# Six small loads in place of two for one input vector of a decode kernel on one core

## The chip, the cores and the metric

The kernel runs on one core of a Trainium2 chip. Its time is the device time of one execution in microseconds (us). A profiled execution also has a span: from its first instruction to its last. The core has five engines with instruction streams of their own: PE (matrix products), DVE (vector operations), ACT (activation functions), POOL and SP. Data is moved by 16 DMA engines; SP and ACT each have one DMA queue (q1 is SP's, q10 is ACT's), and one load of several rows is spread over the DMA engines. A load tells that it has landed by counting up a semaphore.

## The reference, cut to what matters

One token is decoded: attention over a cache with 32 query heads on 4 key/value heads, beside a small two-layer mixer with an MLP; both read the normalised input and are added to the input.

```python
x  = A_x                                   # (1, 1, 1024), bf16
xn = layernorm(x)
q  = (xn @ wq)                             # 32 heads of 128
p  = softmax(q k^T * 128**-0.5)            # 4 key/value heads, 65536 keys each
A  = (p v) @ wo                            # wq: 1024 x 4096, wo: 4096 x 1024
h  = gelu(layernorm(xn) @ w1)              # four groups of channels shifted along the sequence,
x1 = xn + shifted(h) @ w2                  # which has length 1
B  = x1 + gelu(layernorm(x1) @ w3) @ w4    # w3: 1024 x 3584, w4: 3584 x 1024
out = x + A + B                            # (1, 1, 1024)
```

Keys and values are 4 x 65536 x 128 bf16 each. Together with the weights some 170 MB are read once; nothing of it is read twice.

## The kernel before, in words

**Items and slots.** Everything large goes through three slots of 64 KB per partition (pool `big`, `SLOTS = 3`). The list `items` (lines 83 to 89) holds the order: wq, K(0,0), V(0,0), w3, w12 (that is w1 and w2 in one slot), then K and V of the remaining halves of each key/value head, w4 ahead of the last V, and wo in three items. K(g,r) is half r of head g: 32768 keys, 256 per partition, so that one load has 128 rows of 65,536 bytes. The loop of lines 440 to 442 computes item i after it has issued the loads up to item i+2 (`ensure`, `LOOKAHEAD = 2`). All these loads stand in SP's stream (line 119), in the order of the list. A load into a slot waits until the item that had the slot before is consumed: w3 waits for wq's products (line 242), w12 for K(0,0)'s, K(0,1) for V(0,0)'s products (line 393), V(0,1) for w3's, K(1,0) for w12's. A scheduling layer derives these waits from the tiles that each instruction reads and writes; within an engine it keeps the order of issue.

**Semaphores of the loads.** The same layer gives DMAs eight semaphores in turn, in the order in which it meets them. A DMA whose semaphore was used before waits for the earlier DMA on it, unless its engine is known to have waited for that already. At the end SP waits for all of them, two per instruction, in a fixed order (line 468), and then for the other engines.

**The start.** ACT issues two loads of the vector x, ahead of everything else it does: line 123 loads it as 128 rows of 8 elements into `x_bf`; line 130 loads it again as 4 rows of 256 elements into partitions 0, 32, 64 and 96 of `x_q`, which is a part of the tile `work`. That load waits for the memset of line 129. `ones_f`, a matrix of ones, is another part of the same tile, filled by POOL on line 147; the layer takes the four-row load and this memset for overlapping, so that the memset waits for the load. `layernorm` (lines 168 to 188) is a chain over DVE, PE and ACT: the sum over partitions is a product with `ones_f` (lines 172 and 181). It is done twice, the second time on the first one's result. Between the two, DVE does line 199, which scales `x_q`, the only reader of `x_q`; PE adds its result to the accumulator `psB` on line 201. In DVE's stream line 199 stands ahead of lines 174 to 187 of the second layernorm, and in PE's stream line 201 stands ahead of line 181 of the second layernorm and of the products with wq (line 242).

**A key/value half.** `compute_K`: DVE transposes the slot in place in four pieces (line 337), PE multiplies with the queries (line 340), DVE, PE and DVE find the maximum (lines 344 to 355), ACT takes the exponential (line 357), DVE transposes it (line 359). `compute_V`: PE multiplies with the values (line 393). w3 and w12 are computed after V(0,0).

**The end.** The last products with wo go into `psB` (line 161), DVE copies it out (line 435), and SP stores 4 rows of 512 bytes (line 436).

Of the kernel before, what the change touches and what calls it, by code (L numbers as in the profile page):

```python
# [22 lines left out]
def kernel(  # L23
# [14 lines left out]
    nc = tc.nc  # L38
    P = 128
# [8 lines left out]
    DC = D // P  # L48
# [10 lines left out]
    NQ = NOUT // 4  # L59
# [33 lines left out]
    def work():  # L93
        return ppool.tile([P, HF * 512], BF16, name="work")[:]
# [25 lines left out]
        st[item] = t  # L120

    x_bf = const.tile([P, DC], BF16, name="x_bf")
    nc.scalar.dma_start(out=x_bf[:], in_=A_x[0, 0, :].rearrange("(p c) -> p c", c=DC))
    wk0 = work()
    qrow = wk0[:, 0:1024].rearrange("p (b n) -> p b n", b=2)
    psel = wk0[:, 1024:1536].rearrange("p (b m) -> p b m", b=4)
    x_q = wk0[:, 1536:1536 + NQ]
    ones_f = wk0[:, 1792:2048].bitcast(F32)
    nc.vector.memset(x_q, 0.0)
    nc.scalar.dma_start(out=x_q[0:P:32, :], in_=A_x[0, 0, :].rearrange("(j n) -> j n", j=4))  # L130

    n_issued = [0]

# [34 lines left out]
    def layernorm(src, tag):  # L168
# [50 lines left out]
                          in_=sel8[:].unsqueeze(2).to_broadcast([P, 8, 4]))  # L219

    iv = ident_bf[:].rearrange("p (b i r) -> p b r i", b=2, r=2)
    for b in range(2):
        for par in range(2):
            nc.vector.tensor_copy(out=psel[:, 2 * b + par, :].rearrange("p (a i) -> p a i", a=4),
                                  in_=iv[:, b, par, :].unsqueeze(1).to_broadcast([P, 4, 32]))
# [4 lines left out]
                          in_=lead.unsqueeze(2).to_broadcast([P, 4, 16]))  # L230
    gsel = const.tile([P, P], BF16, name="gsel")
    nc.vector.tensor_copy(out=gsel[:].rearrange("p (j m) -> p j m", j=2),
                          in_=lead[:, 0:2].unsqueeze(2).to_broadcast([P, 2, 64]))
# [239 lines left out]
```

## Time and profile before

| | before |
|---|---|
| median of 3 runs | 402.89 us (402.79 to 403.63) |
| the profiled execution | 402.66 us |
| its span | 400.9 us, so 1.8 us lie around it |
| read from memory | 169.87 MB, 424 GB/s over the span |
| busy: PE / DVE / ACT / POOL | 204.0 / 209.0 / 27.3 / 5.9 us |
| mean granted clock of PE | 0.796 |

The busy times are shares of one span of 400.9 us, spread over stages with different limits; the page of the profile also gives the chain of work that ended last, the span in 40 slices, the DMA queues with their packets, and per load the time from its issue to its landing. Line numbers are those of the kernel before; in the changed kernel everything after the first load stands one to three lines lower down.

### The profile page before, as it was taken

The numbers are of one execution on the slowest core, as the hardware profiler recorded it, in microseconds if no ns is written. First come the engines' busy times: TensorE is split into PE (matmuls) and PEld (weight loads), VectorE is DVE, ScalarE is ACT, GpSimd is POOL, SyncE is SP. The second block draws the span as 40 slices with busy tenths as digits, with TensorE's granted clock in tenths as the row PEclk, the third lists the DMA queues.
The fourth block names the chain that finished last, engine by engine and source line by source line (L and its number), as shares of the span: only waits on it lengthen the run. The fifth ranks groups of instructions, "written<-read, shape, count | busy, mean of one in ns | idle before, by whom it ended". The sixth has DMA issues, their size and how long they took to land.

```text
span 400.9 us, 3366 instructions
## 1 busy us (share of the span) xinstructions
PE 204.0 (51%) x1489; PEld 85.4 (21%) x1489; DVE 209.0 (52%) x190; ACT 27.3 (7%) x33; POOL 5.9 (1%) x27
## 2 busy tenths in 40 slices
PE   0016393660079148741965295529453935496235
PEld 0003131220023013310322042204121412143113
DVE  0022992230196559634954894279358841885120
ACT  0002002110000300020002000100200020002000
POOL 1010000000000000000000000000000000000000
PEclk9999698695569587967895689679975976599588
DMA  9999999999999999999999999999999999999994
GB/s 406 425 425 419 419 420 452 401 489 419 425 433 419 419 484 427 419 432 438 420 419 471 432 420 438 438 420 438 451 419 425 433 445 436 419 455 419 414 416 174
DMA packets 3773, 170.07 MB, mean 424 GB/s; under 512 B 552, under 2 KB 560, under 8 KB 816
## 3 DMA queue, kind: packets, MB, share of 16 engines
q1 hardware_dynamic: 3608, 169.87, 98.1%
q8 instruction: 11, 0.18, 0.2%
q10 hardware_dynamic: 152, 0.00, 0.0%
q14 instruction: 2, 0.02, 0.0%
HBM read 169.87 MB, written 0.00 MB: 424 GB/s over the span
## 4 chain that ended last, share of the span: by engine, by line
DMA 48%; PE 26%; DVE 20%; ACT 4%; issue 1%; ACTq 0%; SPq 0%; POOL 0%; DVEq 0%
DMA slot<-in_A_k_cache_dram 28%; PE sc L340 14%; DVE slot L337 12%; DMA slot<-in_A_v_cache_dram 10%; PE oacc L393 8%; DMA work<-in_A_x_dram 7%; DMA slot<-in_A_wo_dram 3%; DVE work L359 3%; DVE mx L344 3%; ACT work L357 3%; PE rows L242 1%; ACT L357 1%; PE pm_mx L346 0%; DVE m L348 0%; DVE og L408 0%
## 5 line engine op out<-in xcount | busy, mean ns | idle before, releaser
L340 PE MATMUL sc<-slot,qst 128*128 128x512 bf16 x512 | 129.8, 415 | 75.6 <-DVE slot L337 75.6
L337 DVE STREAM_TRANSPOSE slot<-slot 128x4096 f32<-128x4096 f32 x32 | 139.4, 4413 | 49.4 <-DMA slot<-in_A_k_cache_dram 49.3
L340 PEld LDWEIGHTS <-qst 128*128 128x128 bf16 x512 | 52.1, 103 | 152.1 <-DVE slot L337 55.9
L393 PE MATMUL oacc<-slot,work 128*32 128x512 bf16 x512 | 43.3, 513 | 45.3 <-DVE work L359 35.7
L344 DVE TENSOR_REDUCE mx<-sc 128x1 f32<-128x2048 f32 x8 | 18.3, 2292 | 30.2 <-PE sc L340 30.2
L393 PEld LDWEIGHTS <-work 128*32 128x32 bf16 x512 | 16.3, 124 | 69.2 <-DVE work L359 36.3
L357 ACT ACTIVATE work<-sc,nball 128x2048 bf16<-128x2048 f32 x8 | 15.7, 1967 | 193.5 <-DVE nball L355 193.5
L359 DVE STREAM_TRANSPOSE work<-work 128x2048 bf16<-128x2048 bf16 x8 | 18.5, 2311 | 19.1 <-ACT work L357 19.1
L408 DVE SCALAR_TENSOR_TENSOR og<-oacc,wm,og 128x128 f32<-128x128 f32 x16 | 5.6, 351 | 22.2 <-PE oacc L393 21.8
L172 PE MATMUL pm_ln<-ln_rowsum_a,work 128*128 128x1 f32 x2 | 0.6, 362 | 27.7 <-POOL work L147 27.7
L166 DVE CAST xT<-x_bf 128x8 f32<-128x8 bf16 x1 | 0.2, 172 | 22.0 <-DMA x_bf<-in_A_x_dram 22.0
L346 PE MATMUL pm_mx<-ident_f,mx 128*1 128x128 f32 x8 | 2.3, 283 | 18.1 <-DVE mx L344 18.1
L242 PE MATMUL rows<-slot,xpad 128*32 128x512 bf16 (+1 forms) x144 | 9.6, 397 | 0.9 <-DMA slot<-in_B_w_dram 0.9
L161 PE MATMUL psB<-slot,oT 128*1 128x256 bf16 x128 | 6.3, 362 | 6.3 <-DMA slot<-in_A_wo_dram 6.1
L357 ACT ACT_TABLE_LOAD x2 | 2.6, 1283 | 73.5 <-DVE nball L355 73.5
L287 DVE TENSOR_TENSOR work<-pm_h,mask 128x448 f32<-128x448 f32 x1 | 0.6, 625 | 11.4 <-PE pm_h L284 11.4
L172 PEld LDWEIGHTS pm_ln<-ln_rowsum_a,work 128*128 128x128 f32 x2 | 0.5, 310 | 27.6 <-POOL work L147 27.6
L435 DVE CAST work<-psB 97x256 bf16<-97x256 f32 x1 | 0.4, 425 | 11.4 <-PE psB L161 11.4
L161 PEld LDWEIGHTS <-oT 128*1 128x1 bf16 x128 | 3.9, 108 | 8.8 <-issue 5.6
L242 PEld LDWEIGHTS <-xpad 128*32 128x32 bf16 x144 | 4.4, 103 | 5.7 <-DMA slot<-in_B_w_dram 1.8
L346 PEld LDWEIGHTS pm_mx<-ident_f,mx 128*1 128x1 f32 x8 | 0.6, 79 | 21.9 <-DVE mx L344 21.9
L412 PE MATMUL pm_e<-og,sel8x 128*32 128x129 f32 x8 | 1.6, 282 | 6.6 <-DVE og L408 6.6
(102 smaller groups left out, 65.4 us busy)
## 6 DMA issues: line engine op xcount, KB each, us to landing
slot<-in_B_w_dram SPq DMA_DIRECT2D x2, 7168.0 KB, 37.7
slot<-in_A_wo_dram SPq DMA_DIRECT2D x1, 5120.0 KB, 27.0
slot<-in_B_w_dram SPq DMA_DIRECT2D x2, 2048.0 KB, 23.1
slot<-in_A_wo_dram SPq DMA_DIRECT2D x1, 2048.0 KB, 26.3
slot<-in_A_wo_dram SPq DMA_DIRECT2D x1, 768.0 KB, 13.5
slot<-in_A_wo_dram SPq DMA_DIRECT2D x1, 256.0 KB
slot<-in_A_k_cache_dram SPq DMA_DIRECT2D x8, 41.7
slot<-in_A_v_cache_dram SPq DMA_DIRECT2D x8, 38.6
```

The lines of the kernel that those rows point to most:

```text
L161: nc.tensor.matmul(psB[32 * j:32 * j + 1, 0:NQ], lhsT=lhsT, rhs=w_row[:, NQ * j:NQ * (j + 1)], start=False, stop=False, tile_position=(0, ...
L172: nc.tensor.matmul(pm[:, 0:1], lhsT=ones_f, rhs=rowsum[:], start=True, stop=True)
L242: nc.tensor.matmul(acc[32 * j:32 * j + 32, bk, 0:width], lhsT=xp[:, c, :], rhs=wt[:, c, ch * width:(ch + 1) * width], start=(c == 0), stop ...
L337: nc.vector.transpose(out=kf[:, cg, :], in_=kf[:, cg, :])
L340: nc.tensor.matmul(sc[:, hf, :], lhsT=qst[g % 2][:, bp, 24 - 8 * cg:24 - 8 * cg + P], rhs=kr[:, cg, hf, :, bp // 2, :, bp % 2], start=(cg ...
L344: nc.vector.reduce_max(out=mx[:], in_=sc[:].rearrange("p h n -> p (h n)"), axis=AX.X)
L346: nc.tensor.transpose(pm[0:1, 0:P], mx[:, 0:1], ident_f[:])
L357: nc.scalar.activation(out=pT, in_=sc[:], func=ACTF.Exp, bias=nball[:, r:r + 1], scale=SCALE, accum_out=lall[:, r:r + 1])
L359: nc.vector.transpose(out=pT, in_=pT)
L393: nc.tensor.matmul(oacc[32 * u:32 * (u + 1), :], lhsT=pT[:, hf, 32 * t:32 * (t + 1)], rhs=vt[:, :, hf, t, :], start=(hf == 0 and t < 4), s ...
L408: nc.vector.scalar_tensor_tensor(out=og[:, 0:P], in0=oacc[:, P * cg:P * (cg + 1)], scalar=wm[:, 1, cg:cg + 1], in1=og[:, 0:P], op0=ALU.mul ...
L412: nc.tensor.matmul(pe[rows, 0:P + 1], lhsT=sel8x[:], rhs=og[:], start=True, stop=True, tile_position=(0, 32 * g))
```

## The change

The load of `x_bf` is split into two loads of 64 rows, and the load of `x_q` into four loads of one row each. The bytes, their source and their places are the same. All six are issued by ACT, in the order written.

```diff
     x_bf = const.tile([P, DC], BF16, name="x_bf")
-    nc.scalar.dma_start(out=x_bf[:], in_=A_x[0, 0, :].rearrange("(p c) -> p c", c=DC))
+    for hp in range(2):
+        nc.scalar.dma_start(out=x_bf[64 * hp:64 * hp + 64, :],
+                            in_=A_x[0, 0, 512 * hp:512 * hp + 512].rearrange("(p c) -> p c", c=DC))
...
     nc.vector.memset(x_q, 0.0)
-    nc.scalar.dma_start(out=x_q[0:P:32, :], in_=A_x[0, 0, :].rearrange("(j n) -> j n", j=4))
+    for j in range(4):
+        nc.scalar.dma_start(out=x_q[32 * j:32 * j + 1, :], in_=A_x[0, 0:1, NQ * j:NQ * (j + 1)])
```

In the built program no instruction of PE, DVE, POOL or SP is added, removed or moved. What differs beside the six loads are the waits. The store is the 28th DMA before and the 32nd after, so it counts on the eighth semaphore in place of the fourth; the loads of SP's stream shift by four places in the same way. The third load of SP's stream, V(0,0), now waits for the first half of `x_bf`; w1 waits for the second half, w2, K(0,1), V(0,1) and K(1,0) for the four rows of `x_q`, one each. Line 166 waits for two loads, line 199 for four. POOL's memset of line 147 no longer waits for a load.

## The prediction

> **What bounds the kernel now.** I read first the slices and the DMA queues of the page.
>
> ```profile
> DMA  9999999999999999999999999999999999999994
> DMA packets 3773, 170.07 MB, mean 424 GB/s; under 512 B 552, under 2 KB 560, under 8 KB 816
> q1 hardware_dynamic: 3608, 169.87, 98.1%
> q10 hardware_dynamic: 152, 0.00, 0.0%
> ```
>
> The DMA engines are busy in every slice, 98.1% of the span for SP's queue alone: the kernel ends when 170 MB have been moved, and a delay of compute costs nothing until SP's queue runs dry. Then every idle microsecond of the DMA engines is lost. So two questions decide: when do the small loads land, and does a late one let q1 run dry?
>
> The packet counts say how loads are cut. q1 has 25 loads and a store: 25 x (128 rows + 16) + 4 + 4 = 3608, so each row is one packet and each DMA engine that takes part adds one for the semaphore. q10: 128 + 16 for `x_bf`, 4 + 4 for `x_q` (on four engines): 152.
>
> Next, the issues of the first 2 us with their time to landing, and the chain of waits.
>
> ```profile
> x_bf<-in_A_x_dram ACTq DMA_DIRECT2D x1, 2.0 KB, 22.3
> slot<-in_A_wq_dram SPq DMA_DIRECT2D x1, 22.1
> ```
>
> ```profile
> 1.18 26.16 DMA work<-in_A_x_dram
> 27.34 0.05 issue
> 27.39 0.21 POOL work L147
> 27.61 0.04 issue
> 27.65 0.60 PE pm_ln L172 x2
> ...
> 34.44 4.48 PE rows L242 x64
> ```
>
> 2 KB need 22.3 us, as long as the 8 MB beside them. The trace's packet records say why: on each DMA engine a packet of q10 goes only between two packets of q1. One engine's 16-byte packets start at 4.83, 7.25, 9.67, 12.09, 14.53, 16.95, 19.37 and 21.79, behind the eight 65,536-byte packets of wq, which take 2.42 us each. Its ninth, the semaphore, goes at 21.80, directly behind wq's own semaphore packet, which is short. `x_q`'s rows follow at 24.34 to 24.57 and their semaphores at 26.78 to 27.02, behind the first and second packet of K(0,0); they land at 27.34. So a q10 packet costs one **turn** of 2.42 us, and turn n goes behind the n-th packet of q1.
>
> ```profile
> 32.40 0.40 DVE L199 TENSOR_SCALAR work<-work,ln_s,ln_s 128x256 f32<-128x256 bf16 x1
> 32.99 1.20 PE L201 MATMUL psB<-work,ident_f 128*128 128x256 f32 x2
> 33.98 0.46 PE L181 MATMUL pm_ln<-ln_rowsq_b,work 128*128 128x1 f32 x2
> 34.37 4.50 PE L242 MATMUL rows<-slot,xpad 128*32 128x512 bf16 x64
> ```
>
> This timeline shows what stands behind `x_q`: line 199 at 32.40, and 2.0 us later the products with wq, which cannot pass line 201 in PE's stream.
>
> Last, SP's own timeline and the chain from the first V onwards.
>
> ```profile
> 38.94 25.26 SPq L119 DMA_DIRECT2D slot<-in_B_w_dram  x3
> 78.67 0.33 SPq L119 DMA_DIRECT2D slot<-in_A_k_cache_dram  x1
> 82.75 0.33 SPq L119 DMA_DIRECT2D slot<-in_A_v_cache_dram  x1
> ```
>
> The tightest place is K(0,1), issued at 78.67, when V(0,0) is consumed. The load queued ahead of it, w2, ends on the 16 DMA engines between 87.14 and 88.72 by the packet records. All other issues have more ahead of them: w3 (38.94) has V(0,0) in flight to 61, w12 (63.4) has w3 to 78, later ones 10 us and more.
>
> **The change part by part.**
>
> *The x_bf halves.* 64 rows over 16 engines are 4 packets and a semaphore: turns 1 to 5 and 6 to 10. Turn 10 goes behind K(0,0)'s first packet, at 24.3 on most engines and 25.0 on the last; with 0.4 us from packet to landing the second half lands near 25.4 in place of 23.0. The memset of line 147 no longer waits, so the first product with ones starts near 25.8 instead of 27.65: 1.9 us are gained here, and they are worth nothing, because line 199 is late next.
>
> *The x_q rows.* Each is one row and one semaphore. No row of this trace shows on which engine a one-row load goes. From one side: all on one engine (or each cut over all 16), 8 turns, 11 to 18. From the other: four engines side by side, turns 11 and 12, landing near 29.6. I take the first, since the loads stand in one queue in the order written and the four rows of one load before took four engines in order. Turn 17 goes behind K(0,0)'s eighth packet, which ends between 41.12 and 41.86, and turn 18 directly behind its short semaphore packet. With 0.3 us to landing: 41.9, against 27.34.
>
> The Trainium skill (DMA: Bandwidth & Descriptors, Why a DMA increments its semaphore by 16 and not by 1) has a load that is not split over all engines run on the lowest-numbered ones, which would put four one-row loads on the same engine.
>
> *What x_q holds up.* Line 199 starts at 41.9, not 32.40: 9.5 us late. Behind it on DVE stand the second layernorm's lines; in 2.0 us, as before, PE gets to the products with wq. K(0,0) landed at 42.19, just when DVE was ready for it (line 337 at 42.24), so nothing later absorbs the delay: the chain from line 242 to V(0,0)'s last product moves as it is. ACT waits for four more semaphores ahead of its first line 357; at 0.07 us for two of them that is 0.1. K(0,1) is issued at 78.67 + 9.5 + 0.1 = 88.3.
>
> *q1 runs dry.* From issue to moving: wq was issued at 0.74 and its first packets ended between 4.83 and 5.59, so less 2.42 they moved effectively 1.67 to 2.43 us after issue. The engine that gets dry first (87.14) is the one at 1.67; it moves again at 88.3 + 1.7 = 90.0, a loss of 2.8 us. It matters that this engine ended late: the packet records show three DMA engines at the end at 396.79 to 396.97, each having done two 16 KB fetches of instructions on the way (0.9 us each); the other thirteen end 0.9 to 2.9 us sooner. Two of the three had their first fetch ahead of 87 us and get dry at 88.7, losing only 1.3; the third is the one above. End: 396.79 + 2.8 = 399.6 against 396.97: **+2.6 us**.
>
> *New waits in SP's stream.* V(0,0) waits for the first half of `x_bf`: turn 5 is 14.5, landing 15. Behind it in SP's stream is w3, which isn't due before 48, and the engines have K(0,0) until 41: nothing. w1 waits for the second half, w2 and the next three for `x_q`'s rows, all landed by 42 and these loads due from 72 on: nothing. If that cover were gone, dry time would be the price, 1 for 1.
>
> *The store's semaphore.* SP's five waits at the end stand 0.066 us apart (399.81 to 400.07), and the store's is in the first of them before, in the last after. Four pass ahead of the landing: **-0.26 us**. The six issues on ACT (0.40 for the first one of before, 1.04 for the second) end by some 6 us at most, and only `x_bf`'s halves have a turn by then: nothing.
>
> Sum: 402.66 + 2.6 - 0.26 = **405.0 us**. The profiled execution is 0.23 us under the median of the runs shown, so beside that median it reads 405.2; I keep 405.0.
>
> Bounds: the delay of 9.5 is 9.3 to 10.0 (which engine takes the rows). Restart is 1.03 us (the first packet's start after its issue) to 2.43. The lost time is 1.3 if the two engines that are late anyway set the end, and 3.9 with the late ends of both. So 403.7 to 406.3, and 0.5 more on top for PE's clock: 403.7 to 406.8.
>
> **The rivals.**
>
> *Side by side.* The four rows go to four engines. `x_q` lands near 29.6, line 199 starts near 30.6 on the gained 1.9 us, and nothing is late. In general all is covered while K(0,1) is issued before 87.14 - 1.7 = 85.5, 6.7 us of delay after the 0.1 on ACT: `x_q` landing before 39.1. Then only the tail counts: 402.4, not slower. For it: the one load of four rows did run on four engines at once. Against it: it was one load.
>
> *Turns hold several packets.* If the DMA engines took several small packets in one turn, six loads would need six turns, be there by 20, and the time would be 402.4 too. Against it: all 152 packets of q10 went one per turn.
>
> The Trainium skill (DMA: Bandwidth & Descriptors, Queues, rings and completion order) has each DMA engine go round its queues and drain a whole packet, typically 9 to 17 descriptors, per visit; by that, `x_bf` before would have landed near 5. The trace differs (22.3 us).
>
> The same page (Anatomy of one DMA) gives some 2.0 us fixed per load; four more loads would then bring `x_q` to an estimated 35.3, and the time to 402.4. The trace has 4.3 us between the two landings (23.02 and 27.34).
>
> *V(0,0) held past K(0,0).* Were the first half of `x_bf` to land after 41.3 - 1.7 = 39.6, q1 would be dry there as well: a landing at 42 costs 2.4, together 407.4. Against it: turn 5.
>
> *The dry time made good later.* The slices rule this out: there is no idle DMA time from which to make it good.
>
> **How the numbers follow.** Forecast 0.68; side by side 0.14; several packets or a smaller fixed price 0.08; V(0,0) held or a longer stall 0.07; else 0.03. About 0.2% (0.8 us) is what a measurement of this kernel can tell from no change. The forecast's own range is 403.7 to 406.8; with 0.22 at 402.4, the range has to take those in: 402.3 to 406.8. Faster by over 0.2% has only the rest and scatter: 0.04. Within: 0.22 and the edge of the forecast: 0.23. Slower: 0.73.
>
> **What would show it.** q10 would have 168 packets (288 if each row is cut over 16 engines). `x_q`'s last row lands near 42, line 199 and the products with wq are 9.5 us later, while the first product with ones is 1.9 us earlier. V(0,0) is issued near 15, K(0,1) near 88, and the slice there falls below 9. I would be wrong if line 199 starts before 39, or if K(0,1)'s landing isn't later than 108.42.

## The result, and the profile after

The changed kernel takes 408.16 us (median; 407.76 to 409.14), the kernel before 402.86 us in the same comparison (402.79 to 403.63): a ratio of 1.0132, 95% interval 1.0117 to 1.0147. It is slower by 5.3 us, on the side that was forecast, but above the range, where the prediction had put 0.07 for a longer stall. The profiled execution took 408.03 us, with a span of 406.1 us and a mean granted clock of 0.802.

The page of the changed kernel, slices and DMA queues:

```profile
DMA  9999998969999999999999999999999999999994
DMA packets 3789, 170.07 MB, mean 419 GB/s; under 512 B 568, under 2 KB 576, under 8 KB 832
q1 hardware_dynamic: 3608, 169.87, 97.3%
q10 hardware_dynamic: 168, 0.00, 0.0%
```

q10 has 16 packets more, the semaphores of the second half. The bytes are the same and the mean rate is lower: the DMA engines stood still somewhere, and the 6 in the slices puts it between 81 and 92 us.

The chain of waits of the changed kernel around `x_q` (start us, us, what):

```profile
3.23 40.87 DMA work<-in_A_x_dram
...
44.22 0.42 DVE work L202
...
44.69 1.22 PE psB L204 x2
...
46.13 4.81 PE rows L245 x64
```

Line 202 is line 199 of before. It started at 32.40 and now starts at 44.22, released by the last row of `x_q`, which lands at 44.09. SP's own timeline shows what follows from it:

```profile
17.73 0.33 SPq L119 DMA_DIRECT2D slot<-in_A_v_cache_dram  x1
50.95 25.25 SPq L119 DMA_DIRECT2D slot<-in_B_w_dram  x3
90.84 0.33 SPq L119 DMA_DIRECT2D slot<-in_A_k_cache_dram  x1
```

K(0,1) is issued at 90.84 instead of 78.67. By the packet records the load ahead of it (w2) ends on the 16 DMA engines between 87.66 and 89.54, and K(0,1)'s first packets start at 91.81 to 92.20. In between q1 is dry. How much the DMA engines moved in the 40 us around this is read from the table by stretch (us, busy time of PE, PEld, DVE, ACT and POOL, clock, DMA share, GB/s). Before:

```profile
60.00:100.00 40.00, 16.59 (x197) 6.98 (x195) 8.97 (x11) 6.72 (x7) 0.53 (x1) 0.76 1.02 441
```

and after:

```profile
60.00:100.00 40.00, 26.77 (x211) 10.98 (x209) 20.27 (x13) 6.72 (x7) 0.52 (x1) 0.84 0.93 383
```

58 GB/s less over 40 us are 2.32 MB, and at the mean of 424 GB/s of the kernel before that is 5.5 us. This is rough, since the view counts a packet whole where it starts (so the DMA share can read 1.02). With each packet shared out over its duration the records give 432 GB/s before and 375 after, which is 5.3 us. The store lands 5.45 us later (405.24, 399.79 before). So the whole loss arises here, and nothing later gives any of it back.

### The profile page after: what moved, and what is told of

Read it like the earlier page. It is cut to its first block, busy times and chain, and to the rows that moved or that the text cites. A ratio compares the mean times of both kernels' runs of the same rounds, so it can differ in the third digit from the quotient of the medians.

```text
span 406.1 us, 3376 instructions
## 1 busy us (share of the span) xinstructions
PE 206.6 (51%) x1489; PEld 86.7 (21%) x1489; DVE 208.7 (51%) x190; ACT 27.3 (7%) x33; POOL 5.8 (1%) x27
## 4 chain that ended last, share of the span: by engine, by line
DMA 49%; DVE 23%; PE 22%; ACT 3%; issue 1%; ACTq 1%; SPq 0%; DVEq 0%
DMA slot<-in_A_k_cache_dram 26%; DVE slot L340 15%; PE sc L343 11%; DMA work<-in_A_x_dram 10%; DMA slot<-in_A_v_cache_dram 10%; PE oacc L396 9%; DMA slot<-in_A_wo_dram 4%; DVE work L362 3%; DVE mx L347 3%; ACT work L360 3%; PE rows L245 1%; ACT L360 1%; PE pm_mx L349 0%; DVE m L351 0%; DVE og L411 0%
## 5 line engine op out<-in xcount | busy, mean ns | idle before, releaser
L340 DVE STREAM_TRANSPOSE slot<-slot 128x4096 f32<-128x4096 f32 x32 | 139.4, 4414 | 41.9 <-DMA slot<-in_A_k_cache_dram 41.8
L396 PE MATMUL oacc<-slot,work 128*32 128x512 bf16 x512 | 45.0, 529 | 45.4 <-DVE work L362 35.7
L204 PE MATMUL psB<-work,ident_f 128*128 128x256 f32 x2 | 1.2, 714 | 11.6 <-DVE work L202 11.6
```

The source lines that it names most:

```text
L204: nc.tensor.matmul(psB[:, 0:NQ], lhsT=ident_f[:], rhs=accx, start=True, stop=False, skip_group_check=True)
L340: nc.vector.transpose(out=kf[:, cg, :], in_=kf[:, cg, :])
L396: nc.tensor.matmul(oacc[32 * u:32 * (u + 1), :], lhsT=pT[:, hf, 32 * t:32 * (t + 1)], rhs=vt[:, :, hf, t, :], start=(hf == 0 and t < 4), s ...
```

## The experiments

All were measured against the kernel before on the same chip: 402.94 us (402.72 to 403.11) beside the first four, 402.95 us (402.69 to 403.37) beside the others. The table goes ahead of the details; "first" is the start of the first small packet, "row" the landing of the last row of `x_q`, all in us from the span's start. Span and events are those of the profiled execution. K(0,1)'s issue moves by more than the row where PE's clock rises later under the products in between (4.48 to 6.10 us for the 64 with wq); the part on the prediction shows this.

| | packets of q10 | first | row | K(0,1) issued | span | median | ratio (95%) |
|---|---|---|---|---|---|---|---|
| before | 152 | 4.83 | 27.34 | 78.67 | 400.9 | 402.94, 402.95 | 1 |
| after | 168 | 7.29 | 44.09 | 90.84 | 406.1 | 408.16 | 1.0132 (1.0117 to 1.0147) |
| e1_bf_halves | 168 | 7.23 | 32.03 | 83.75 | 401.0 | 402.82 | 0.9997 (0.9988 to 1.0007) |
| e2_q_rows | 152 | 4.67 | 41.91 | 89.22 | 404.9 | 407.12 | 1.0099 (1.0081 to 1.0116) |
| e3_late_reader | 168 | 7.25 | 44.24 | 79.90 | 400.9 | 402.92 | 0.9998 (0.9989 to 1.0007) |
| e4_small_rows | 280 | 7.29 | 46.59 | 98.61 | 414.7 | 416.31 | 1.0327 (1.0311 to 1.0342) |
| e5_spare_16rows | 280 | 4.78 | 27.30 | 80.04 | 401.0 | 403.05 | 1.0000 (0.9991 to 1.0009) |
| e6_spare_1row | 160 | 4.79 | 27.31 | 80.93 | 400.9 | 403.07 | 1.0002 (0.9993 to 1.0011) |
| e7_three_parts | 184 | 7.22 | 34.45 | 87.08 | 403.2 | 404.94 | 1.0049 (1.0037 to 1.0062) |
| e8_sp_later | 168 | 2.05 | 34.80 | 81.25 | 401.4 | 403.32 | 1.0009 (0.9999 to 1.0018) |

**e1_bf_halves**: the kernel before with the first part of the change alone, `x_bf` in two halves.

```diff
-    nc.scalar.dma_start(out=x_bf[:], in_=A_x[0, 0, :].rearrange("(p c) -> p c", c=DC))
+    for hp in range(2):
+        nc.scalar.dma_start(out=x_bf[64 * hp:64 * hp + 64, :],
+                            in_=A_x[0, 0, 512 * hp:512 * hp + 512].rearrange("(p c) -> p c", c=DC))
```

> Only x_bf is split (two loads of 64 rows); x_q stays one load of four rows. Theory of turns (each packet of ACT's queue waits behind one packet of SP's queue on its DMA engine): 10 packets of x_bf and 2 of x_q per engine, so x_q lands behind the third or fourth packet of K(0,0), at 29.4 (31.9 if the first turn is missed, as in the changed kernel). The first product with ones then starts 2 to 4.5 us late, K(0,1) is issued before 84 and the DMA engines do not get dry: 402.6 to 402.9. Rival, a fixed price per load (5.4 us for four loads): 404.2. Rival, the new semaphore waits in SP's stream: no such wait ahead of w3, so no change.

```profile
83.75 0.33 SPq L119 DMA_DIRECT2D slot<-in_A_k_cache_dram  x1
```

The time is that of before. One load more brought one turn more ahead of `x_q` (ten instead of nine), and the turns began one late, so the row lands at 32.03, 4.7 us later than before. K(0,1) is issued 5.1 us later, and q1 did not run dry: by the packet records K(0,1)'s first packets start from 87.08 on, directly behind w2. The halves alone are covered.

**e2_q_rows**: the second part alone.

```diff
-    nc.scalar.dma_start(out=x_q[0:P:32, :], in_=A_x[0, 0, :].rearrange("(j n) -> j n", j=4))
+    for j in range(4):
+        nc.scalar.dma_start(out=x_q[32 * j:32 * j + 1, :], in_=A_x[0, 0:1, NQ * j:NQ * (j + 1)])
```

> Only x_q is split (four loads of one row); x_bf stays one load. Theory of turns: 9 + 8 packets, the 17th behind the last packet of K(0,0) (if a turn is missed the 18th place, directly behind K(0,0)'s short semaphore packet, so the same time): x_q lands at 41.7, line 199 starts near 41.9, K(0,1) is issued near 88.5 and the DMA engines stand still for about 3 us: 405.6. Rival, a fixed price per load: three more loads, 406.9. Rival, the waits in SP's stream: V(0,0) waits for nothing here, so 402.7.

```profile
2.36 39.55 DMA work<-in_A_x_dram
...
42.04 0.42 DVE work L200
```

```profile
60.00:100.00 40.00, 26.48 (x231) 11.17 (x233) 18.83 (x14) 6.72 (x7) 0.52 (x1) 0.84 0.93 394
```

The landing (41.91) is the expected one, and the number of q10's packets is that of before: there are no more packets, but the same eight stand on one DMA engine instead of four. SP issues V(0,0) at 1.65 here, as before, so a wait ahead of V(0,0) is not needed for the loss. The time came out 1.5 us above the expectation: K(0,1) was issued 0.7 later than expected (chiefly because the products with wq took 5.19 us instead of 4.48), the time around the span was 0.35 longer, and the rest is a dry time 0.4 longer than reckoned. By its time alone, the rival of a fixed price per load (406.9) comes nearer than the 405.6; it is the landing at the expected place, and e1 and e4, that decide against it. The rate from 60 to 100 us is 394 GB/s; 47 less than before for 40 us are some 4.4 us. The slices of this kernel show a 9 throughout but for the last: here the rate shows the dry queue, and the slice doesn't.

**e3_late_reader**: all six loads as in the changed kernel, the same waits in SP's stream, but `x_q` in a tile of its own, and its reader moved behind the computation of w3's layer.

```diff
-    x_q = wk0[:, 1536:1536 + NQ]
+    x_q = const.tile([P, NQ], BF16, name="x_q")[:]
...
-    accx = wk0[:, 0:2 * NQ].bitcast(F32)
-    nc.vector.tensor_scalar(out=accx, in0=x_q, scalar1=ln_s1[:, 0:1], scalar2=ln_s2[:, 0:1],
-                            op0=ALU.mult, op1=ALU.add)
-    nc.tensor.matmul(psB[:, 0:NQ], lhsT=ident_f[:], rhs=accx, start=True, stop=False, skip_group_check=True)
+    def add_x():
+        accx = work()[:, 0:2 * NQ].bitcast(F32)
+        ...
+        nc.tensor.matmul(psB[:, 0:NQ], lhsT=ident_f[:], rhs=accx, start=True, stop=False, skip_group_check=True)
...
+        add_x()
```

> The six loads of the changed kernel, with the same semaphores and the same waits in SP's stream; x_q has a tile of its own and its reader (line 199 with the product of line 201) stands behind the computation of w3. Theory of turns: the last row still lands near 44, but nothing waits for it until 90; the layernorm starts near 27.5 on the earlier memset, K(0,1) is issued near 78, nothing gets dry and the tail keeps its 0.25: 402.4. Rival, the waits in SP's stream or a price of the loads themselves: 408 as in the changed kernel.

In DVE's timeline the reader now stands here:

```profile
86.38 0.41 DVE L203 TENSOR_SCALAR work<-x_q,ln_s,ln_s 128x256 f32<-128x256 bf16 x1
```

and in SP's timeline:

```profile
17.79 0.33 SPq L119 DMA_DIRECT2D slot<-in_A_v_cache_dram  x1
...
79.90 0.33 SPq L119 DMA_DIRECT2D slot<-in_A_k_cache_dram  x1
```

```profile
60.00:100.00 40.00, 18.18 (x200) 7.49 (x198) 9.91 (x13) 6.72 (x7) 0.52 (x1) 0.78 1.02 441
```

The rows land as late as in the changed kernel (44.24), and V(0,0) waits as long (17.79), yet the rate from 60 to 100 us is that of before, and so is the time. So the late landing costs only through its reader's place in DVE's and PE's streams; the six issues, their packets and SP's waits cost nothing in themselves. The expected gain at the tail isn't in the time: see below.

**e4_small_rows**: two loads as before, no wait added, but each row of `x_bf` is cut into two pieces of 8 bytes, by a gap in the tile.

```diff
-    x_bf = const.tile([P, DC], BF16, name="x_bf")
-    nc.scalar.dma_start(out=x_bf[:], in_=A_x[0, 0, :].rearrange("(p c) -> p c", c=DC))
+    x_bf = const.tile([P, 2, DC], BF16, name="x_bf")
+    nc.scalar.dma_start(out=x_bf[:, :, 0:DC // 2], in_=A_x[0, 0, :].rearrange("(p h c) -> p h c", h=2, c=DC // 2))
...
-    nc.vector.tensor_copy(out=xT[:], in_=x_bf[:])
+    nc.vector.tensor_copy(out=xT[:].rearrange("p (h c) -> p h c", h=2), in_=x_bf[:, :, 0:DC // 2])
```

> Two loads as in the kernel before, with the same semaphores and waits, but x_bf is stored with a gap so that each of its 128 rows is two packets of 8 bytes: 16 packets and a semaphore per DMA engine. Theory of turns: x_bf lands at 41.7, x_q two turns later at 44.1 (46.5 if a turn is missed); POOL's memset and the first product with ones wait for it, 16.8 us late (19.2), K(0,1) is issued near 95.5, and the DMA engines stand still for 10 us (12.5): 412.9 (415.3). Rival, a fixed price per load: no more loads, so 402.9. Rival, the waits in SP's stream: none added, 402.9.

```profile
q10 hardware_dynamic: 280, 0.00, 0.0%
```

```profile
1.43 45.16 DMA work<-in_A_x_dram
...
98.61 22.78 DMA slot<-in_A_k_cache_dram
```

The same 2 KB by the same number of loads cost 13.4 us more, two and a half times the loss of the change. The first turn was missed here too, so the expectation's second figure, 415.3, holds; the time is 1.0 us above it. This settles the unit of the price: with one load more the row lands 4.7 us later (e1), with no load more but eight packets more per DMA engine 19.3 us later. The price is not the load's, but the packet's on one DMA engine.

**e5_spare_16rows and e6_spare_1row**: `x` by two loads as before; behind them four spare loads into a tile that nobody reads, so that the number of DMAs and SP's semaphores are those of the changed kernel.

```diff
+    spare = const.tile([P, NQ], BF16, name="spare")
...
+        if (g, r) == (1, 0):
+            for j in range(4):
+                nc.scalar.dma_start(out=spare[0:16, 16 * j:16 * j + 8],
+                                    in_=A_x[0, 0, 128 * j:128 * j + 128].rearrange("(p c) -> p c", c=8))
```

In e6 each is one row instead: `spare[32 * j:32 * j + 1, :]` from `A_x[0, 0:1, NQ * j:NQ * (j + 1)]`. The lines stand in `compute_K`, but ACT issues the four from 2.29 and 2.31 us on, directly behind `x_q`: the order of the text isn't kept for them.

> x is loaded by two loads as in the kernel before. Behind them ACT issues four more small loads (16 rows of 16 bytes each) into a tile that nothing reads. That gives 32 DMAs: SP's stream, its semaphores and its waits are those of the changed kernel, the store's place in the last of SP's waits included. Theory of turns: the spare loads stand behind x in ACT's queue, x_q lands at 27.3 as before, nothing is late; from the store's landing to the end of the span 0.84 us in place of 1.09, and a time of 402.7 beside 402.94, if the end of the span is the end of the time. Rival, the new waits in SP's stream: 408.

> As the kernel with four spare loads, but each is one row of 512 bytes, as in the changed kernel. Theory of turns: as there, 402.7. In the three kernels with one-row loads so far, the time was 1.94 to 2.15 us over the span, in the others 1.80: if the one-row loads themselves do that, this kernel shows it (402.9 with a span of 400.9) and the one with 16-row loads does not.

Both take the time of before, with `x_q` at 27.3. V(0,0) waits for all of `x_bf` (it is issued at 22.98 in e5, at 23.07 in e6), and it costs nothing. With e3 this rules out SP's waits as the cause. The 402.7 expected wasn't reached: the span came out as expected, but the time around it is longer, in e5 as much as in e6, so it isn't the one-row loads that lengthen it (see below).

**e7_three_parts**: `x_bf` in 64, 32 and 32 rows, `x_q` by one load; a delay between e1's and e2's, to find where the cover ends.

```diff
-    nc.scalar.dma_start(out=x_bf[:], in_=A_x[0, 0, :].rearrange("(p c) -> p c", c=DC))
+    for p0, n in ((0, 64), (64, 32), (96, 32)):
+        nc.scalar.dma_start(out=x_bf[p0:p0 + n, :],
+                            in_=A_x[0, 0, DC * p0:DC * (p0 + n)].rearrange("(p c) -> p c", c=DC))
```

> x_bf in three loads (64, 32 and 32 rows), x_q in one: 11 + 2 packets per DMA engine, one turn more than with two halves. Theory of turns: x_q lands at 34.3 (31.9 with two halves), K(0,1) is issued near 86.2 (83.75). This lies just behind the point at which the DMA engines get dry, which the runs so far put at an issue near 85.2: 403.9, that is 1.0 us slower than before. Rival, a fixed price per load of 1.35 us (the changed kernel's 5.4 over four loads): 405.6. Rival, waits in SP's stream: none ahead of w1, 402.9.

```profile
87.08 0.33 SPq L119 DMA_DIRECT2D slot<-in_A_k_cache_dram  x1
```

One turn more than in e1 and the row lands 2.4 us later, as expected. K(0,1) is issued 0.9 us later than expected, because the products with wq and with V(0,0) took 5.45 and 6.20 us (4.84 and 5.89 in e1), and the time is 2.0 us above that of before instead of 1.0. Issue less loss gives the point from which it costs: by the store's landing in the profiled executions it is 84.7 here, 85.0 in e2, 85.4 in the changed kernel and 84.8 in e4. e1 with 83.75 lies below it and loses nothing. The forecast had put this point at 85.5.

**e8_sp_later**: the changed kernel, with a spare load of one row ahead of wq in SP's stream, so that wq is issued at 1.15 instead of 0.74. It was to give ACT's first load its first turn back.

```diff
+    spare = const.tile([P, DC], BF16, name="spare")
+    nc.sync.dma_start(out=spare[0:1, :], in_=A_x[0, 0:1, 0:DC])
```

> The changed kernel, but SP first issues a spare load of one row of 16 bytes, so that wq is issued some 0.3 us later. What it tests: why the first small packet went behind the second 65,536-byte packet and not the first. If it is that ACT's first issue took 0.55 us in place of 0.40 and came too late for the first turn, it is in time here: x_q's last row lands at 41.9 in place of 44.1 (plus the 0.3 of wq), K(0,1) is issued near 89, and the time is near 406.5. If six loads lose that turn for another reason, the time is 408.2 or more.

```profile
3.22 31.59 DMA work<-in_A_x_dram
...
34.93 0.42 DVE work L204
...
81.25 27.82 DMA slot<-in_A_k_cache_dram
```

It gave back nearly four turns (9.3 us), not one. Each DMA engine took the first half's four data packets and its semaphore one after the other between 2.05 and 2.33, ahead of wq's first packet. The first half landed by 2.7, the last row at 34.80 instead of 44.09, and K(0,1) was issued at 81.25, on the covered side. The time is 0.37 us above that of before, about what wq was issued later; the interval just includes no change. A turn is thus the price of a packet behind a queue that is already moving; ahead of that queue five packets together took 0.3 us at most.

## Why the prediction was wrong in size and right in mechanism

By the profiled executions 408.03 - 405.0 = 3.0 us are missing. The mechanism is the one forecast; the term of the sum that was too small is the dry time, +2.6 us, which measured 5.45. Most of that lies in one step ahead of it.

*`x_q`'s landing: 44.09, not 41.9 (+2.2).* **This is the step that failed**: turn 1 was put behind the first packet of wq, as before, and it went behind the second (7.29 us instead of 4.83). From there on the 18 turns came as reckoned, one place later. The four rows went one after the other on one engine: the records of the changed kernel show data at 29.18, 34.04, 38.89 and 41.34, and semaphores at 31.62, 36.47, 41.33 and 43.78; the pair at 41.33 and 41.34 is the short place behind K(0,0)'s semaphore. Whether the four rows would share an engine was the open question of the prediction. The records name no engine, but all other steps are 2.42 to 2.44 us, the turn of one engine, so they do. The rule of the Trainium skill that spoke for it (DMA: Bandwidth & Descriptors, Why a DMA increments its semaphore by 16 and not by 1) agrees with these records, as far as one engine goes; which number it has they don't show.

Why a turn was missed is in the first microseconds of ACT's timeline. Before:

```profile
0.74 0.40 ACTq L123 DMA_DIRECT2D x_bf<-in_A_x_dram  x1
0.74 0.39 SPq L119 DMA_DIRECT2D slot<-in_A_wq_dram  x1
```

and after:

```profile
0.74 0.37 SPq L119 DMA_DIRECT2D slot<-in_A_wq_dram  x1
0.74 1.19 ACTq L124 DMA_DIRECT2D x_bf<-in_A_x_dram  x2
```

Of the 1.19 us, the first half's issue takes 0.55 by the chain of waits. Wherever the first load on ACT was the one of 128 whole rows (before, e2, e5, e6), its issue took 0.40 to 0.42 and the first small packet came at 4.67 to 4.83. Wherever it was 64 rows or cut rows (after, e1, e3, e4, e7), it took 0.54 to 0.66, and the packet came at 7.22 to 7.29, one 2.42 us turn later. SP's issue of wq stands beside it at 0.37 to 0.39. The prediction counted the six issues as "nothing", by their end at some 6 us, and did not ask which packet of wq they would still catch. e8 moves the other side of this race by 0.4 us and the landing by 9.3 us. What decides within those 0.1 us, the trace doesn't show. In e8 the first small packets came 1.3 us after ACT's issue began; with the same 1.3 us they would have been there near 2.1 in the changed kernel too (an estimate), well before wq's first packets ended at 4.88 to 5.30, and still they went behind its second.

*Line 199 to K(0,1)'s issue (+0.35).* 46.27 us before, 46.62 after, where 0.1 was foreseen; the start behind the landing adds 0.13. The 64 products with wq took 4.48 us before, 4.81 after, and 4.61 to 6.10 in the experiments; those with V(0,0) 5.71 before, 5.87 after, and 5.78 to 6.52. PE's clock decides this: in the trace's clock records full clock first stands 1.71 us behind the start of the products with wq before, 2.37 us after and 4.99 us in e6, and each microsecond later cost 0.5 us of product time, in all ten traces to within 0.02. (The views take the clock as full ahead of the first record.) Under the products with V(0,0) the clock rises from half to full 4.17 us behind their start before, 4.51 us after and 5.82 us in e6, at the same price. The prediction took this stretch as rigid and allowed 0.5 us for the clock in the range alone.

*Dry time (+0.3).* For an issue at 90.84 the prediction's own rule gives some 5.2 us; 5.45 were lost. Its 1.67 us from issue to moving is 1.6 to 2.2 by the records: K(0,1)'s first packets start 0.97 to 1.36 us after the issue and take 3.03 to 3.51 us, where a later one takes 2.42. One place more was tight than the prediction saw: w1's first packets start from 77.4 on, directly behind w3, and on seven engines the first of 16 KB takes 1.6 to 2.5 us, where none took more than 1.2 there before. It should add nothing, because the queue ran dry behind it anyway and then waited for K(0,1)'s issue; no run tests it alone.

*The store's semaphore: right in the span, not in the time (+0.15).* From the store's landing to the end of the span 1.09 us pass before, 0.83 after, the forecast -0.26. But what lies around the span is longer: 1.79 us before (median of 27 runs), 1.95 after, 2.03 in e3, 2.15 to 2.17 in e2, e5 and e6, 1.76 to 1.82 in e1, e4 and e7. So e5 and e6, whose median span of 400.9 is 0.3 under that of before beside them (401.2), aren't shorter in time (403.05 and 403.07, beside 402.95), and the gain is gone. The kernels with 31 DMAs or more (after, e2, e3, e5, e6, e8) have the longer time around the span, those with up to 30 don't. The trace shows nothing outside the span; the cause stays open.

*The memset that no longer waits.* It is free, but the first product with ones starts at 28.03, not 25.8:

```profile
27.52 0.17 DVE L169 CAST xT<-x_bf 128x8 f32<-128x8 bf16 x1 [26.52 <-DMA x_bf<-in_A_x_dram]
```

The second half landed at 27.42, the missed turn again (25.4 forecast). V(0,0)'s issue at 17.73 (near 15 forecast) is late by the same turn. Neither matters, as forecast.

*The rivals.* Side by side falls by the one engine above. Several packets per turn falls by the turns of the changed kernel and by e4; a fixed price per load by e1 against e4. The 2.0 us per load that the prediction takes from the Trainium skill stand there for loads that POOL issues, while these are ACT's; no run here shows such a price. V(0,0) held past K(0,0) falls by 17.73. That SP's new waits cost nothing is shown by e3, e5 and e6, and that nothing is made good later by the store's landing.

No version beat the kernel before: e1, e3, e5, e6 and e8 equal it within the interval.

## What to carry to other kernels

Behind a stream of large packets, price a small load by its packets on the busiest DMA engine, times the duration of one large packet, and not by its bytes or by the number of loads; splitting rows that ran on four engines into loads of one row puts them on one. Then ask who reads it first, and how far that reader can slip before the next large load is issued too late: here some 6 us were free (from 78.67 to a point between 84.7 and 85.4), and each microsecond past them was lost. Small loads that must be there early belong ahead of the large stream (e8: 34.80 instead of 44.09), and a count of turns needs the first turn checked, since it can shift by a whole large packet.

## What the runs showed of the hardware

- A difference of 0.12 us or more in the issue of ACT's first load went with one whole turn (2.42 us) for the first packet of its queue, in nine kernels out of nine with wq issued at 0.74; starting wq 0.4 us later brought the last small row 9.3 us earlier.
- In the changed kernel the dry queue effectively moved again 1.6 to 2.2 us after the issue; 0.6 to 1.1 us of it are a first packet that takes longer (3.03 to 3.51 us instead of 2.42).
- The same 64 products took 4.48 to 6.10 us as PE's clock became full 1.71 to 4.99 us behind their start.
- The time around the span isn't constant: 1.76 to 2.17 us between kernels that differ by a few small DMAs.
